# An attention and gated feed-forward kernel: the planner counts TensorE's waits as instructions, and works the order out anew

## The chip, the cores and the metric

The kernel runs on one core of one Trainium2 chip. The metric is device microseconds of one execution. Before the change three runs took 560.89, 561.74 and 563.44 us, median 561.74. A further execution was profiled: it took 564.12 us itself, and its span, from the first to the last instruction, is 562.3 us.

## The reference

Eight batches, eight heads, head size 64. 512 local positions see each other in a band and 32 global positions in full; the global positions see everything. The result, transposed to 576 x 512 per batch, goes through a product with a 512 x 1024 weight, a convolution of three taps along the sequence as a gate, and a product with a 1024 x 512 weight.

```python
s_g = scale * q_g @ k_all.T            # 32 global queries, all 544 keys
out_g = softmax(s_g) @ v_all
s_ll = where(abs(i - j) <= 32, scale * q_l @ k_l.T, -1e9)
s_l = concat([scale * q_l @ k_g.T, s_ll])
out_l = softmax(s_l) @ concat([v_g, v_l])
x = transpose(concat([out_g, out_l]))   # batch, 576, 512
h = max(x @ w_in, 0)
conv = sum(conv_w[k] * shifted(h, k - 1) for k in range(3))
out = (h * sigmoid(conv)) @ w_out
```

All of it is fp32. The weights come as float64.

## The kernel before

**Attention.** Heads go in pairs, 32 pairs in all, four to a batch. A step is one function call for one pair, head or group, and the planner names it by a letter. S (`SC`, line 270) makes the scores of a pair with 64 small matmuls of 32 columns of weights each (in the first batch also two masks by line 275). M, NM, E, NS, NP and TD are maximum, scaling, exponential, sums, division and a 32 x 32 transposition on VectorE, ScalarE or GpSimd. P (`PV`, line 367) multiplies by the values with 104 small matmuls; UA copies the result out of PSUM. Once a batch the global queries take G (line 296, 48 small matmuls), GM, GE, GN, GT (transpositions, lines 426 and 427), GC, GP (line 441, 80 small matmuls), GD, GX and GO.

**Feed-forward.** It goes in nine chunks: the 512 local columns of each batch, and a last one with the 35 columns a batch that are left (280). A chunk has eight Z steps (`PZ`, line 476): each is 12 matmuls of 128 x 512, four blocks of channels times three products of split operands. In chunk 0 a Z step is 4 plain fp32 matmuls (line 471, eight records). RE, C1, Ca, Cb, TH, GG, GH and GL are rectifier, convolution, tanh gate and split of the result on ScalarE and VectorE. Four output blocks follow, each in two halves Oa and Ob (line 530) of 12 full-width matmuls. OE copies an output block to SBUF and ST stores it. The float64 weights, eight loads of 1024 KB (WD), are turned into fp32 and split by WA, WB, WC, WH and WL in the first part of the kernel. A load of a pair's queries and keys (LQ) has 704 KB, one of its values (LV) 448 KB.

**The order.** Nothing is ordered by hand. `plan` (line 696) lists all steps with costs, buffers and dependences, and gives each a due time: TensorE steps from `attention` and `feed` (lines 782 and 790), which read the table TIME, plus a shift from POS0 (first batch and weights), POS1 (second batch) or POS; other steps from what needs them, less SLACK times the costs between, plus a shift. `arranged` (line 863) plays the five engines' queues through in time: whenever an engine is free it takes the ready step with the earliest due time for which the buffers are free. The start times so found give the order, which `emit` (line 954) writes out and fixes on every engine. So the numbers in the tables change the order and nothing else of the program.

**TensorE's program as the planner sees it.** Every matmul has a weight load as an instruction of its own. `INSTR` (line 685) and `instructions` (line 689) give the number of instructions of a step: 128 for S, 208 for P, 96 for G, 160 for GP, 24 for a full-width group of 12 matmuls. In `arranged` (lines 922 to 928) the program is cut in blocks of 256, the first boundary at 190. Some instructions ahead of a boundary the fetch of the block after it is begun; it is there some time later, and a step that reaches a boundary before its block is there is late by the difference. Separate waits (`EVENT_SEMAPHORE`), which the compiler puts into TensorE's program where an instruction waits for more than it can name, are not counted.

Of the kernel before, what the change touches and what calls it, by code (L numbers as in the profile page):

```python
# [19 lines left out]
P = 128  # L20
H = 8
SL = 512
SG = 32
S = SL + SG
# [39 lines left out]
def attn_moe(ctx: ExitStack, tc: tile.TileContext, qk_d, vw_d, qg_d, w_in_d, w_out_d, cw_d, out_d):  # L64
# [269 lines left out]

    def NP(n):
        p, r = heads[n]["p"], heads[n // 2 * 2]["r"][:, n % 2]
        if choice("NP") == "a":
            for t in range(4):
                nc.scalar.activation(out=p[:, t], in_=p[:, t], func=AF.Copy, scale=r[:, t : t + 1])  # L339
        else:  # L340
            eng("NP").tensor_tensor(out=p, in0=p, in1=r[:, :, None].to_broadcast([P, 4, P]), op=ALU.mult)

# [33 lines left out]

    def XE(n):
        b, h = divmod(n, H)
# [42 lines left out]

    def GT(n):
        gr = groups[n // 4]
# [115 lines left out]
    def ST(o):  # L539
# [9 lines left out]
    emit(tc, B, dict(  # L549
        LQ=LQ, LV=LV, LG=LG, G=G, S=SC, M=MA, NM=NM, E=EX, NS=NS, NP=NP, TD=TD, P=PV, UA=UA, XE=XE, XH=XH, XL=XL,  # L550
        GM=GM, GE=GE, GN=GN, GT=GT, GC=GC, GP=GP, GD=GD, GX=GX, GO=GO,
# [12 lines left out]
ENG = dict(  # L564
    GC="a", GO="a", NP="a", XH="a", XL="p", NM="a", RE="a", C1="a", GH="v", GL="v", OE="v", UA="a", GD="a",
    WH="a", WL="v",
)
ENG0 = dict(
    GC="a", GO="a", NP="p", XH="a", XL="v", NM="a", RE="a", C1="a", GH="a", GL="v", OE="a", UA="a", GD="a",
    WH="a", WL="v",  # L570
)

POS = dict(
    XE=-1.98, LQ=-80.99, LG=-87.83, LV=71.12, S=-17.28, M=-27.44, E=-6.13, NS=-3.92, NM=23.86, P=1.39, UA=-4.24,
    NP=31.47, TD=-5.07, XH=-12.07, XL=10.02, G=52.87, GM=29.81, GE=-37.35, GN=-115.2, GD=105.99, GX=29.95,
    GT=129.43, GC=-31.93, GP=-26.41, GO=-8.78, PZ=14.19, RE=-3.14, C1=2.98, Ca=0.43, Cb=0.55, TH=9.34, GG=-5.2,
    GH=8.26, GL=-12.28, Oa=61.51, Ob=-1.61, OE=61.39, ST=-10.74, WD=-19.78, TP=-9.03, WA=-50.95, WB=133.34, WC=0.26,
    WH=37.69, WL=-74.11,
)
POS0 = dict(  # L580
    XE=71.87, LQ=7.24, LG=-63.06, LV=45.31, S=126.77, M=-117.38, E=8.85, NS=-300.71, NM=-150.66, P=-86.58,
    UA=-59.52, NP=-71.33, TD=-53.52, XH=39.01, XL=-39.39, G=-5.17, GM=-83.24, GE=24.98, GN=-203.07, GD=23.65,
    GX=12.62, GT=31.6, GC=-44.1, GP=68.52, GO=-255.02, PZ=107.21, RE=31.17, C1=13.3, Ca=-9.79, Cb=-16.57, TH=-79.02,
    GG=-97.16, GH=-0.63, GL=9.06, Oa=110.77, Ob=0.43, OE=-108.95, ST=93.13, WD=-24.99, TP=-179.51, WA=78.67,
    WB=8.55, WC=-17.88, WH=37.31, WL=7.82,
)
POS1 = dict(
    XE=-150.52, LQ=4.25, LG=21.89, LV=64.47, S=-102.2, M=55.36, E=-44.06, NS=-77.31, NM=-31.46, P=51.55, UA=-82.55,
    NP=17.29, TD=-25.06, XH=12.69, XL=-16.47, G=199.57, GM=-62.58, GE=148.46, GN=17.3, GD=81.6, GX=-42.37,
    GT=112.38, GC=-31.9, GP=-31.58, GO=-202.72, PZ=98.05, RE=-16.73, C1=124.35, Ca=-6, Cb=127.63, TH=14.86,  # L590
    GG=160.89, GH=79.39, GL=44.16, Oa=-177.1, Ob=11.66, OE=142.4, ST=7.86, WD=-94.15, TP=28.9, WA=53.39, WB=-5.7,
    WC=103.86, WH=35.99, WL=96.74,
)

TIME = dict(
    A0=35.78, R0=-44.3, A1=35.35, R1=-21.21, A2=113.9, R=14.48, PER=62.4, T0=117.37, Z0=-24.44, O0=74.74, OR0=9.08,
    T1=118.03, ZR=178.55, OD=30.59, OR=19.82, END=-27.04,
)
MASKED = 1
SLACK = 2.092  # L600

WAYS = {}

# [1 line left out]
def cost(key, e, long=LONG):  # L605
# [45 lines left out]
    if key == "C1":  # L651
        return act(n, more=93) if e == "a" else fast(n) if e == "v" else pool1(n)
    return dict(
        LQ=dma(704), LV=dma(448), LG=dma(64), WD=dma(1024), ST=(900, 2400),
        S=pe(940), SM=pe(1400), M0=(690, 770), XE=(110, 140), TD=(590, 670), P=pe(1430), G=pe(940), GT=pe(500), GP=pe(1190), GX=pe(150),
        PZ=group(), Oa=group(), Ob=group(), F=pe(3540),
# [18 lines left out]
    p=("S", "G", "GT", "P", "GP", "GX", "PZ", "Oa", "Ob"), s=("LQ", "LV", "LG", "WD", "ST"),  # L675
    a=("E", "GE", "TH", "WA"), g=("XE",),
)
PE, DVE, ACT, POOL, SP = range(5)
# [4 lines left out]


INSTR = dict(S=128, P=208, G=96, GT=10, GP=160, GX=2)
FETCH = (190, 3400, 64)


def instructions(key, i):

    if key == "PZ" and i < NFT:
        return 16
    return INSTR.get(key, 24) + 4 * (key == "S" and i < H * MASKED)


def plan(B):
# [166 lines left out]
def arranged(ops):  # L863

    free = {k: v for k, v in SLOTS.items()}
    free["h"], free["o_"], free["at"] = LIMIT["h"], LIMIT["o"], LIMIT["at"]
    kind, left, gone = {}, {}, {}
    for key, i, e, c, takes, uses, before, pos, later in ops:
        for k, name in takes:
            kind[name] = k  # L870
            left[name] = left.get(name, 0) + 1
        for name in uses:
            left[name] = left.get(name, 0) + 1
    after = [[] for _ in ops]
    waits = [0] * len(ops)
    for j, o in enumerate(ops):
        waits[j] = len(o[6])
        for x in o[6]:
            after[x].append(j)
    ready = [0] * len(ops)  # L880
    queue = [[] for _ in range(5)]
    for j, o in enumerate(ops):
        if not waits[j]:
            queue[o[2]].append(j)
    until, shared, mode = [0] * 5, 0, 0
    begun, bound, trigger, there, coming = 0, FETCH[0], FETCH[0] - FETCH[2], 0, 0
    start = [None] * len(ops)
    events, done, now = [0], 0, -1
    frees = []
    while events:  # L890
        t = heapq.heappop(events)
        if t == now:
            continue
        now = t
        while frees and frees[0][0] <= t:
            free[heapq.heappop(frees)[1]] += 1
        for e in (PE, DVE, ACT, POOL, SP):
            if until[e] > t:
                continue
            best = None  # L900
            for j in queue[e]:
                o = ops[j]
                at = o[7] - (STAY if e == PE and mode and MODE.get(o[0], 0) == mode else 0)
                if ready[j] > t or (best is not None and (at, j) >= best):
                    continue
                if (e == POOL or (e == DVE and o[0] in SHARED)) and shared > t:
                    continue
                need = {}
                for k, _ in o[4]:
                    need[k] = need.get(k, 0) + 1  # L910
                if all(free[k] >= v for k, v in need.items()):
                    best = (at, j)
            if best is None:
                continue
            j = best[1]
            key, i, _, (occ, lat), takes, uses, before, pos, later = ops[j]
            queue[e].remove(j)
            if e == PE:
                m = MODE.get(key, 0)
                if m != mode:  # L920
                    occ, lat, mode = occ + SWITCH[m > 0], lat + SWITCH[m > 0], m
                count, late = instructions(key, i), 0
                while min(trigger, bound) < begun + count:
                    at = t + late + occ * (min(trigger, bound) - begun) // count
                    if trigger < bound:
                        coming, trigger = max(at, there) + FETCH[1], trigger + 256
                    else:
                        late, there, bound = late + max(there - at, 0), coming, bound + 256
                begun, occ, lat = begun + count, occ + late, lat + late
            start[j] = t  # L930
            done += 1
            until[e] = t + occ
            heapq.heappush(events, t + occ)
            if e == POOL or (e == DVE and key in SHARED):
                shared = t + occ
            for k, _ in takes:
                free[k] -= 1
            for name in [x for _, x in takes] + list(uses):
                gone[name] = max(gone.get(name, 0), t + lat)
                left[name] -= 1  # L940
                if not left[name]:
                    heapq.heappush(frees, (gone[name] + 60, kind[name]))
                    heapq.heappush(events, gone[name] + 60)
            for x in after[j]:
                ready[x] = max(ready[x], t + lat + (20 if ops[x][2] == e else 100 if ops[x][2] == POOL else 45))
                waits[x] -= 1
                if not waits[x]:
                    queue[ops[x][2]].append(x)
                    heapq.heappush(events, max(ready[x], t))
    assert done == len(ops), [ops[j][:2] for q in queue for j in q]  # L950
    return start, max(s + o[3][1] for s, o in zip(start, ops))
# [73 lines left out]
```

## Time and profile before

| | |
|---|---|
| three runs | 560.89, 561.74, 563.44 us |
| profiled execution, its own time | 564.12 us |
| its span | 562.3 us |
| TensorE busy with matmuls | 528.6 us, 94% |
| TensorE weight loads (beside them) | 414.3 us, 74% |
| VectorE busy | 421.8 us, 75% |
| ScalarE busy | 373.8 us, 66% |
| GpSimd busy | 71.7 us, 13% |
| matmuls, weight loads | 8192, 8192 |
| mean granted clock of TensorE | 0.969 |
| data moved by the DMA engines | 56.83 MB |
| packets of the two instruction queues | 64 (1.05 MB) and 21 (0.17 MB) |

The profile is of one execution. "busy" is the union of an engine's instructions in time. A granted clock of 1 is 2.4 GHz and 0.5 is 1.2 GHz. "issue" as the cause of idle time means that the engine waited for no semaphore that the profile shows. In a row of waits the numbers are us in total, times, and the longest. PE is TensorE, PEld its weight loads, DVE VectorE, ACT ScalarE, POOL GpSimd, SP the engine that issues the loads and stores.

### The profile page before, as it was taken

How to read it: one execution, taken by the hardware profiler on the slowest of the kernel's cores; microseconds unless marked ns; L12 is line 12 of the kernel's file. 1: busy time of each engine (PE TensorE's matmuls, PEld its weight loads, DVE VectorE, ACT ScalarE, POOL GpSimd, SP SyncE). 2: the span in 40 equal slices, each digit the busy share in tenths (PEclk: the TensorE clock that was granted, in tenths of full speed). 3: DMA queues.
4: the chain of work that ended last, by engine and by line, in shares of the span. 5: the costliest groups of instructions: out<-in, count | busy, mean ns of one | idle time of the engine just before them, and what ended most of it. 6: DMA issues, size and time to landing. Idle time of an engine off the chain costs nothing.

```text
span 562.3 us, 19172 instructions
## 1 busy us (share of the span) xinstructions
PE 528.6 (94%) x8192; PEld 414.3 (74%) x8192; DVE 421.8 (75%) x796; ACT 373.8 (66%) x1262; POOL 71.7 (13%) x98
## 2 busy tenths in 40 slices
PE   5779899998999998999999998999899999999996
PEld 3465366787778886787878886877777788888895
DVE  2897999998888786674787766897758659667562
ACT  4867976778876794769676784879538865433230
POOL 4412321001210012000400022001300031101000
PEclk9658999999999999999999998999999999999999
DMA  8992651142222304222050404240030000000112
GB/s 344 417 358 77 230 189 64 54 141 94 100 89 72 115 30 151 76 97 100 23 188 38 175 3 152 71 174 23 26 113 21 4 35 6 37 20 19 39 39 38
DMA packets 20517, 56.83 MB, mean 101 GB/s; under 512 B 6096, under 2 KB 11216, under 8 KB 19408
## 3 DMA queue, kind: packets, MB, share of 16 engines
q1 hardware_dynamic: 20432, 55.61, 27.5%
q8 instruction: 64, 1.05, 0.8%
q14 instruction: 21, 0.17, 0.1%
HBM read 46.69 MB, written 8.91 MB: 99 GB/s over the span
## 4 chain that ended last, share of the span: by engine, by line
PE 83%; DVE 8%; issue 3%; ACT 3%; DMA 1%; POOL 0%; DVEq 0%; ACTq 0%; POOLq 0%
PE ps_o L530 33%; PE ps_h L476 29%; PE ps_v L367 8%; PE ps_s L270 6%; PE ps_h L471 2%; PE go L441 2%; DVE negm L304 1%; DVE pt L326 1%; PE psg L296 1%; DVE t L496 1%; PE gt L426 1%; ACT pr L339 1%; DMA qk<-qk 1%; ACT pr L316 1%; DVE ps_s L303 1%
## 5 line engine op out<-in xcount | busy, mean ns | idle before, releaser
L530 PE MATMUL ps_o<-g,wh 128*128 128x512 f32 (+1 forms) x576 | 186.6, 392 | 0.0
L496 DVE SCALAR_TENSOR_TENSOR t<-h,cw,t 128x511 f32<-128x511 f32 (+1 forms) x144 | 104.2, 734 | 29.6 <-ACT t L250 28.6
L530 PEld LDWEIGHTS ps_o<-g,wh 128*128 128x128 f32 x576 | 108.0, 190 | 23.6 <-issue 0.8
L530 PE MATMUL ps_o<-g,wl 128*128 128x512 f32 (+1 forms) x288 | 111.0, 385 | 0.0
L476 PE MATMUL ps_h<-h,wh 128*128 128x512 f32 (+1 forms) x256 | 100.9, 394 | 0.0
L476 PE MATMUL ps_h<-h,wl 128*128 128x512 f32 (+1 forms) x256 | 98.0, 383 | 0.0
L476 PE MATMUL ps_h<-l,wh 128*128 128x512 f32 (+1 forms) x256 | 97.5, 381 | 0.0
L316 ACT ACTIVATE pr<-ps_s,negm 128x128 f32<-128x128 f32 x256 | 90.1, 369 | 1.7 <-DVE pt L326 0.7
L484 ACT ACTIVATE h<-ps_h 128x512 f32<-128x512 f32 (+1 forms) x72 | 41.7, 580 | 52.6 <-PE ps_h L476 45.5
L367 PEld LDWEIGHTS ps_v<-pt,vf 32*64 32x64 f32 x3328 | 51.2, 140 | 24.3 <-issue 12.2
L502 ACT ACTIVATE t<-t 128x512 f32<-128x512 f32 (+1 forms) x72 | 44.0, 612 | 34.8 <-DVE t L496 32.4
L367 PE MATMUL ps_v<-pt,vf 32*64 32x64 f32 (+3 forms) x3328 | 57.4, 254 | 10.1 <-issue 5.9
L530 PEld LDWEIGHTS ps_o<-g,wl 128*128 128x128 f32 x288 | 54.7, 190 | 10.8
L326 DVE STREAM_TRANSPOSE pt<-pr 128x512 f32<-128x512 f32 x64 | 44.7, 703 | 23.4 <-ACT pr L339 21.5
L339 ACT ACTIVATE pr<-pr,sums 128x128 f32<-128x128 f32 x192 | 60.8, 407 | 1.7 <-DVE sums L333 1.7
L506 DVE SCALAR_TENSOR_TENSOR t<-t,h 128x512 f32<-128x512 f32 (+1 forms) x72 | 52.8, 742 | 12.1 <-ACT t L502 11.8
L250 ACT ACTIVATE t<-h,cw 128x512 f32<-128x512 f32 (+1 forms) x72 | 50.5, 706 | 13.1 <-DVE g L220 12.4
L476 PEld LDWEIGHTS ps_h<-h,wh 128*128 128x128 f32 x256 | 48.1, 188 | 11.9 <-issue 1.6
L476 PEld LDWEIGHTS ps_h<-h,wl 128*128 128x128 f32 x256 | 48.1, 188 | 10.4
L476 PEld LDWEIGHTS ps_h<-l,wh 128*128 128x128 f32 x256 | 48.1, 188 | 9.3
L304 DVE TENSOR_REDUCE negm<-ps_s 128x4 f32<-128x512 f32 x64 | 44.0, 691 | 12.9 <-PE ps_s L275 10.3
L316 ACT ACTIVATION_READ_ACCUMULATOR pr<-ps_s,negm 128x1 f32 x256 | 53.4, 208 | 0.0
(74 smaller groups left out, 580.0 us busy)
## 6 DMA issues: line engine op xcount, KB each, us to landing
qk<-qk SPq DMA_DIRECT2D x32, 704.0 KB, 6.0
vf<-vw SPq DMA_DIRECT2D x32, 448.0 KB, 4.5
out<-o SPq DMA_DIRECT2D x32, 255.5 KB, 2.0
raw<-w_in SPq DMA_DIRECT2D x4, 1024.0 KB, 11.3
raw<-w_out SPq DMA_DIRECT2D x4, 1024.0 KB, 7.0
out<-o SPq DMA_DIRECT2D x4, 132.0 KB, 3.2
qgf<-qg SPq DMA_DIRECT2D x8, 64.0 KB, 5.7
cwr<-cw SPq DMA_DIRECT2D x1, 24.0 KB, 10.0
```

The costliest lines, as they stand in the source:

```text
L250: nc.scalar.activation(out=out, in_=in_, func=AF.Copy, scale=by)
L304: nc.vector.tensor_reduce(out=st["m"], in_=st["s"], axis=mybir.AxisListType.X, op=ALU.max)
L316: nc.scalar.activation(out=st["p"][:, t, :], in_=st["s"][:, t, :], func=AF.Exp, scale=SCALE, bias=st["m"][:, t : t + 1], accum_out=two["r" ...
L326: nc.vector.transpose(out=st["pt"][:, n % 2].rearrange("p t k q -> p (t k q)"), in_=heads[n]["p"].rearrange("p t k -> p (t k)"))
L339: nc.scalar.activation(out=p[:, t], in_=p[:, t], func=AF.Copy, scale=r[:, t : t + 1])
L367: nc.tensor.matmul(x, lhsT=v, rhs=p, start=k == 0, stop=k == len(work[j, b]) - 1)
L476: nc.tensor.matmul(st["z"][:, 0:n], lhsT=w_in(w, ft, ct), rhs=x[part], start=i == 0, stop=i == 3 * NCT - 1)
L484: nc.scalar.activation(out=h[:, 0:n], in_=z[:, 0:n], func=AF.Relu, scale=0.5)
L496: nc.vector.scalar_tensor_tensor(out=t, in0=h, scalar=cw[:, 3 * ft + k : 3 * ft + k + 1], in1=t, op0=ALU.mult, op1=ALU.add)
L502: nc.scalar.activation(out=t, in_=t, func=AF.Tanh)
L506: nc.vector.scalar_tensor_tensor(out=t, in0=t, scalar=1.0, in1=h, op0=ALU.add, op1=ALU.mult)
L530: nc.tensor.matmul(ps, lhsT=w_out(w, mt, ft), rhs=g, start=ft + i == 0, stop=ft == NFT - 1 and i == 2)
```

## The change

The count of a step's instructions gets one more in P, G and GP steps and in every third of the others. A fetch is taken to last 3450 instead of 3400 ns, or 5500 ns if the queue of loads is still busy in the plan up to 1500 ns before the time at which the fetch begins, and it begins 50 instead of 64 instructions ahead of the boundary. The tables POS, POS0, POS1, TIME and SLACK have new numbers, so the order of all steps on all engines is new. The steps themselves, the buffers, the costs and the engines that they run on stay as they are.

```diff
--- before.py
+++ after.py
@@ -571,33 +571,33 @@
 )
 
 POS = dict(
-    XE=-1.98, LQ=-80.99, LG=-87.83, LV=71.12, S=-17.28, M=-27.44, E=-6.13, NS=-3.92, NM=23.86, P=1.39, UA=-4.24,
-    NP=31.47, TD=-5.07, XH=-12.07, XL=10.02, G=52.87, GM=29.81, GE=-37.35, GN=-115.2, GD=105.99, GX=29.95,
-    GT=129.43, GC=-31.93, GP=-26.41, GO=-8.78, PZ=14.19, RE=-3.14, C1=2.98, Ca=0.43, Cb=0.55, TH=9.34, GG=-5.2,
-    GH=8.26, GL=-12.28, Oa=61.51, Ob=-1.61, OE=61.39, ST=-10.74, WD=-19.78, TP=-9.03, WA=-50.95, WB=133.34, WC=0.26,
-    WH=37.69, WL=-74.11,
+    XE=-40.21, LQ=155.99, LG=44.21, LV=48.17, S=94.27, M=-3.78, E=2.16, NS=-1.35, NM=-2.21, P=-1.79, UA=5.89,
+    NP=-1.47, TD=1.18, XH=-2.94, XL=4.6, G=134.07, GM=50.45, GE=-31.52, GN=-23.16, GD=37.91, GX=-54.56, GT=-11.1,
+    GC=26.27, GP=-0.81, GO=229.47, PZ=33.3, RE=-2.63, C1=-3.89, Ca=4.61, Cb=3.23, TH=-1.63, GG=2.68, GH=-2.01,
+    GL=-2.31, Oa=-12.37, Ob=3.86, OE=-44.57, ST=-7.64, WD=-61.54, TP=3.93, WA=163.45, WB=-95.99, WC=55.97,
+    WH=186.14, WL=-46.68,
 )
 POS0 = dict(
-    XE=71.87, LQ=7.24, LG=-63.06, LV=45.31, S=126.77, M=-117.38, E=8.85, NS=-300.71, NM=-150.66, P=-86.58,
-    UA=-59.52, NP=-71.33, TD=-53.52, XH=39.01, XL=-39.39, G=-5.17, GM=-83.24, GE=24.98, GN=-203.07, GD=23.65,
-    GX=12.62, GT=31.6, GC=-44.1, GP=68.52, GO=-255.02, PZ=107.21, RE=31.17, C1=13.3, Ca=-9.79, Cb=-16.57, TH=-79.02,
-    GG=-97.16, GH=-0.63, GL=9.06, Oa=110.77, Ob=0.43, OE=-108.95, ST=93.13, WD=-24.99, TP=-179.51, WA=78.67,
-    WB=8.55, WC=-17.88, WH=37.31, WL=7.82,
+    XE=-29.14, LQ=-45.12, LG=-169.65, LV=13.98, S=-8.27, M=-87.9, E=-21.95, NS=32.88, NM=27.73, P=76.08, UA=-13.17,
+    NP=13.23, TD=-13.91, XH=-13.93, XL=76.42, G=13.87, GM=-34.75, GE=-12.19, GN=33.78, GD=-85.95, GX=1.77,
+    GT=-97.72, GC=5.1, GP=24.67, GO=-100.45, PZ=2, RE=-8.58, C1=69.32, Ca=72.28, Cb=-17.55, TH=-30.35, GG=-6.29,
+    GH=-31.2, GL=-3.32, Oa=-20.38, Ob=3.35, OE=-9.78, ST=40.96, WD=-45.63, TP=35.8, WA=3.99, WB=-10, WC=5.61,
+    WH=-10.47, WL=1.6,
 )
 POS1 = dict(
-    XE=-150.52, LQ=4.25, LG=21.89, LV=64.47, S=-102.2, M=55.36, E=-44.06, NS=-77.31, NM=-31.46, P=51.55, UA=-82.55,
-    NP=17.29, TD=-25.06, XH=12.69, XL=-16.47, G=199.57, GM=-62.58, GE=148.46, GN=17.3, GD=81.6, GX=-42.37,
-    GT=112.38, GC=-31.9, GP=-31.58, GO=-202.72, PZ=98.05, RE=-16.73, C1=124.35, Ca=-6, Cb=127.63, TH=14.86,
-    GG=160.89, GH=79.39, GL=44.16, Oa=-177.1, Ob=11.66, OE=142.4, ST=7.86, WD=-94.15, TP=28.9, WA=53.39, WB=-5.7,
-    WC=103.86, WH=35.99, WL=96.74,
+    XE=-29.02, LQ=-26.54, LG=-11.72, LV=93.31, S=58.42, M=37.61, E=-2.61, NS=11.38, NM=-11.02, P=-15.31, UA=34.12,
+    NP=-6.55, TD=-11.58, XH=50.36, XL=-98.13, G=55.74, GM=-84.06, GE=76.43, GN=-59.12, GD=-20.14, GX=97.12,
+    GT=-18.53, GC=-1.63, GP=155.32, GO=89.44, PZ=-12.58, RE=59.82, C1=198.55, Ca=75.2, Cb=83.72, TH=-29.44,
+    GG=168.39, GH=-55.2, GL=-1.43, Oa=156.85, Ob=-9.56, OE=-16.45, ST=145.12, WD=-48.91, TP=92.07, WA=-133.55,
+    WB=-219.38, WC=287.43, WH=-48.95, WL=-54.48,
 )
 
 TIME = dict(
-    A0=35.78, R0=-44.3, A1=35.35, R1=-21.21, A2=113.9, R=14.48, PER=62.4, T0=117.37, Z0=-24.44, O0=74.74, OR0=9.08,
-    T1=118.03, ZR=178.55, OD=30.59, OR=19.82, END=-27.04,
+    A0=9.42, R0=27.75, A1=43.69, R1=6.01, A2=101.89, R=15.35, PER=63.73, T0=-59.35, Z0=160.71, O0=74.51, OR0=21.33,
+    T1=104.58, ZR=114.59, OD=23.52, OR=13.58, END=-16.52,
 )
 MASKED = 1
-SLACK = 2.092
+SLACK = 2.025
 
 WAYS = {}
 
@@ -683,14 +683,15 @@
 
 
 INSTR = dict(S=128, P=208, G=96, GT=10, GP=160, GX=2)
-FETCH = (190, 3400, 64)
+FETCH = (190, 3450, 50, 5500)
 
 
 def instructions(key, i):
 
+    waits = key in ("P", "G", "GP") or i % 3 == 0
     if key == "PZ" and i < NFT:
-        return 16
-    return INSTR.get(key, 24) + 4 * (key == "S" and i < H * MASKED)
+        return 16 + waits
+    return INSTR.get(key, 24) + 4 * (key == "S" and i < H * MASKED) + waits
 
 
 def plan(B):
@@ -923,7 +924,8 @@
                 while min(trigger, bound) < begun + count:
                     at = t + late + occ * (min(trigger, bound) - begun) // count
                     if trigger < bound:
-                        coming, trigger = max(at, there) + FETCH[1], trigger + 256
+                        at = max(at, there)
+                        coming, trigger = at + FETCH[3 if until[SP] + 1500 > at else 1], trigger + 256
                     else:
                         late, there, bound = late + max(there - at, 0), coming, bound + 256
                 begun, occ, lat = begun + count, occ + late, lat + late
```

## Rows read from the trace of the kernel before

**Rows 1.** The page's first section: busy us, share of the span, instructions.

```profile
PE 528.6 (94%) x8192; PEld 414.3 (74%) x8192; DVE 421.8 (75%) x796; ACT 373.8 (66%) x1262; POOL 71.7 (13%) x98
```

**Rows 2.** By stretch: length, busy (count) of PE, PEld, DVE, ACT, POOL, clock, DMA, GB/s.

```profile
0.00:44.00 44.00, 29.14 (x856) 21.00 (x856) 28.85 (x62) 28.82 (x121) 15.30 (x34) 0.71 0.93 361
...
84.00:546.00 462.00, 451.94 (x6534) 361.78 (x6533) 350.53 (x653) 309.98 (x1032) 45.38 (x53) 0.99 0.21 73
546.00:562.35 16.35, 10.84 (x84) 10.61 (x83) 4.79 (x11) 1.38 (x3) 0.00 (x0) 0.96 0.21 33
...
343.00:346.00 3.00, 3.00 (x14) 2.25 (x9) 1.15 (x2) 1.74 (x4) 0.56 (x2) 0.50 0.65 189
```

**Rows 3.** TensorE's waits from 84 us on: us in all, times, longest.

```profile
PE ps_s L270 <- issue: 5.0, 3, 2.6
PE go L441 <- issue: 3.3, 2, 1.8
PE ps_v L367 <- issue: 1.5, 1, 1.5
PE ps_v L367 <- DVE o L217: 0.3, 1, 0.3
```

**Rows 4.** TensorE in time order: start, us, work; in brackets idle before.

```profile
134.70 0.24 PE L367 MATMUL ps_v<-pt,vf 32*64 32x32 f32 x1 [1.47 <-issue]
...
218.27 1.57 PE L367 MATMUL ps_v<-pt,vf 32*64 32x128 f32 x104
219.77 1.11 PE L270 MATMUL ps_s<-qk 64*32 64x128 f32 x59
223.52 0.64 PE L270 MATMUL ps_s<-qk 64*32 64x128 f32 x5 [2.64 <-issue]
...
435.93 0.87 PE L270 MATMUL ps_s<-qk 64*32 64x128 f32 x41 [1.09 <-issue]
```

**Rows 5.** By stretch as rows 2, cut at the ends of stops.

```profile
14.10:134.65 120.55, 107.88 (x2032) 74.17 (x2031) 109.60 (x208) 94.23 (x316) 22.40 (x25) 0.89 0.49 183
150.45:223.50 73.05, 70.39 (x1145) 56.14 (x1145) 58.96 (x109) 51.60 (x177) 8.87 (x11) 1.00 0.26 89
14.10:435.92 421.82, 400.53 (x6866) 307.43 (x6866) 338.75 (x648) 311.88 (x1074) 55.29 (x64) 0.96 0.32 115
```

**Rows 6.** Separate waits in TensorE's program, of the P step's line.

```profile
L367 PEldq EVENT_SEMAPHORE  x52: 51/51/51, 17.7 to 458.5; - x52
```

**Rows 7.** Instruction packets: 0 to 44, 84 to 546, 220.8 to 223.6 us.

```profile
q8 instruction: 6, 0.10, 0.9%
...
q8 instruction: 52, 0.85, 0.8%
...
q8 instruction: 1, 0.02, 2.2%
```

**Rows 8.** The chain that ended last: start, us, what.

```profile
215.34 3.00 PE ps_o L530 x12
...
224.16 4.11 PE ps_o L530 x12
...
235.20 2.80 PE ps_o L530 x12
...
343.24 4.30 PE ps_o L530 x12
```

**Rows 9.** TensorE's waits up to 84 us; then the first feed-forward group.

```profile
PE ps_s L270 <- DMA qk<-qk: 5.0, 1, 5.0
PE ps_v L367 <- issue: 4.4, 4, 2.6
PE ps_v L367 <- ACT pr L316: 2.6, 3, 1.4
PE ps_s L270 <- issue: 1.9, 1, 1.9
...
44.67 4.18 PE L471 MATMUL ps_h<-x,wf 128*128 128x512 f32 x8
```

## The prediction, on record before the result

> **What bounds the kernel now.** I read the engine shares first. TensorE is busy for 528.6 of the 562.3 us [rows 1]; VectorE has 421.8 and ScalarE 373.8 us, so only TensorE's sum is near the span. The table by stage [rows 2] then splits TensorE's missing 33.7 us: 14.9 us are missing in the first 44 us, 10.1 in the 462 us between 84 and 546, 5.5 after 546, and so 3.2 between 44 and 84. The granted clock says the same: 0.71 in the first 44 us, 0.99 from 84 to 546, where 1 is 2.4 GHz. So the kernel has an opening of some 84 us with several limits, then a long stretch that TensorE fills, then a short tail.
>
> In the long stretch the waits of TensorE [rows 3] show almost one cause. It waited 0.3 us for VectorE, once, and 9.8 us in six gaps that end with "issue", that is, with no semaphore that the profile shows. Three of the six stand in [rows 4], and all look alike: two or three of the steps with many small matmuls stand directly behind each other (a P step of 104 matmuls, then an S step of 64, in the row that has its run-up), and the engine stops inside one of them: 1.47, 1.28, 2.64, 1.80, 1.52 and 1.09 us in order of time, 9.80 in all.
>
> Why there? Count the instructions from one stop to the next [rows 5]. From 150.45 to 223.50 us there are 1145 matmuls and 1145 weight loads, 2290; 9 x 256 is 2304, 14 more. From the first 256-instruction boundary at which it stops, at 14.1 us, to the first of the six, the sum falls short of 16 x 256 by 33; in the remaining four stretches it does so by 3, 25, 13 and 4. The missing instructions are the separate waits in TensorE's program: there are 104 of them in the whole kernel, by nine rows of which the largest stands in [rows 6], and the shortfalls sum to 92 by 436 us: 2 x 6866 = 13732 against 54 x 256 = 13824 over all six stretches together. So the six stops stand on one grid of 256 instructions, waits included. In the 2.8 us around the 2.64 us stop the DMA records hold just one packet of the instruction queue, of 0.02 MB [rows 7]: the engine stood at the end of a block of its program while the next was being fetched.
>
> The Trainium skill ("Runtime: NRT & Kernel Launch", section "Instruction fetch mechanics") has the same block of 256 instructions, 16 KiB, but says that crossing a boundary is mostly hidden because instructions are dispatched more slowly than fetched. By that rule the gaps would be something else, and a corrected count would save nothing. The trace disagrees with it for runs of small matmuls (2.64 us lost at one boundary) and agrees for the other boundaries, since 52 blocks came between 84 and 546 us [rows 7], and 46 of them cost nothing.
>
> **The planner's old count and the new one.** The old planner has this mechanism already, without the waits: its boundaries drift away from the true ones, by as many instructions as there were waits before. At the six stops those are 33, 36, 50, 75, 88 and 92, by summing [rows 5]. What was left of the run of small matmuls at each stop was 1, 7, 5, 27, 13 and 41 matmuls [rows 4], twice as many instructions: 2, 14, 10, 54, 26, 82. Each is smaller than the drift. So at all six the old planner believed that the boundary lay behind the run, in a full-width group, where 24 instructions last 2.8 us and a fetch is covered. The six stops are not bad luck in the durations; they are the counting error. The new rule adds one for each P, G and GP step and for every third of the other steps: 32 + 8 + 8, and 11 S, 6 GT, 3 GX, 24 PZ, 12 Oa and 12 Ob, 116 in all against 104 measured. The drift shrinks from 104 to about 12 at the end.
>
> **The terms**, against the profiled execution's own 564.12 us (the span and 1.8 us around it). No instruction of the computation is added or removed; the order and the places of the waits change.
>
> 1. The six stops: -9.8 us if none returns. The engine stops where some 300 small instructions stand together (163 matmuls and their loads, 326, before the 2.64 us stop [rows 4]), and the planner can now see which boundaries fall so.
> 2. The clock behind them. Behind the two longest stops it fell: it is 0.50, that is 1.2 GHz, from 343 to 346 us [rows 2], behind the 1.80 us stop. There a group of 12 matmuls took 4.30 us and behind the 2.64 us stop 4.11, where such a group behind small matmuls takes 3.00 [rows 8]. That is 1.1 + 1.3 = 2.4 us, gone with the stops: -2.4.
> 3. Stops that return: a count off by up to 12, and a fetch that can last longer than planned. From 0 to all of terms 1 and 2 (12.2); I take one of six at its mean, +1.6, since the error left is an eighth of the old one.
> 4. Keeping such steps apart. A full-width group lasts 2.80 us behind another and 3.00 behind small matmuls [rows 8], so each run that is broken up costs 0.20 us. Bounds: nothing (runs moved to another place) to 32 P steps apart, 6.4 us; six runs, +1.2.
> 5. The opening, whose order is wholly new: the first parameter set (POS0) and the first chunks' times change by tens of units. TensorE waits there 6.3 us on "issue", 5.0 us for the first load, and 6.8 us on ScalarE and VectorE, in six rows of which the largest stands in [rows 9]. The wait for the first load stays: what TensorE needs first is still a pair's queries and keys. The fetch part should shrink with the new 5.5 us under loads, but the DMA engines are 0.93 busy and only 6 blocks came in the first 44 us [rows 2, 7], 7 us each, which is more than 5.5; and a step freed from the fetch meets the ScalarE and VectorE waits next. Bounds: -6.3 (all of its fetch waits) to +18 (as much again as the 18.1 us that TensorE misses up to 84 us). I take 0, between small gains and small losses, because nothing in the trace shows which way a new order of this stretch goes.
> 6. The waits on other engines between 84 and 546 us: 0.3 us before. TensorE is covered because VectorE is busy 350.5 of 462 us there and ScalarE 310.0 [rows 2], so each has slack, and the planner's costs for them held. 0; if that cover goes, each late result costs what such waits cost in the opening, up to some 0.9 us (2.6 us in three times, [rows 9]).
> 7. The tail, 5.5 us without matmuls at the end, is the last copies and two stores behind each other; the order of the last steps hardly differs in kind. 0, give or take 1.
>
> Sum: -9.8 - 2.4 + 1.6 + 1.2 = -9.4, so 554.7 for the profiled execution. That execution was 2.4 us above the median of the three runs shown (561.74), so the median goes to 552.3; I write 552.4.
>
> **Rivals.**
> The opening gets longer (slower). The place is the first group of chunk 0, which starts at 44.67 us [rows 9] and needs four pairs' attention and the first weights. Loads come at 361 GB/s [rows 2], so each load of 1024 KB that the new order puts ahead of what this group needs moves it 2.9 us. From 3.2 such loads on (9.4 us) all of the gain is gone; with five, four weight loads and more than a pair's queries and keys, it is 14.5 us, and the time 561.7 - 9.4 + 14.5 = 567. For it: the new settings turn the sequence of the first attention pairs round (R0 from -44 to +28). Against it: the old opening was no better ordered by any row that I can see.
>
> The gain is there but is eaten, or the stops only move: the longer fetch time in the plan makes the scheduler hold small-matmul steps back, their results come late, and TensorE waits for ScalarE and VectorE as it does in the opening (6.8 us), plus two of the six stops at 1.6. -9.4 + 6.8 + 3.2 = +0.6, or 562.3, no change. That the change doesn't do what it says belongs here: waits are given to steps by a rule, not read from the program, and 52 of the 104 stand at the P line alone [rows 6], where the rule gives 32, so the boundaries could be off by more in some stretch.
>
> By the rule of a hidden fetch the "issue" gaps come from elsewhere and stay: 561.7 as well, by 9.8 us that do not move. The block grid of [rows 5] speaks against it.
>
> The opening gains too: its 6.3 us go and the first group comes earlier by as much: 552.4 - 6.3 = 546.1.
>
> **Chances and range.** Forecast, from 548 to 557 by itself: 0.60. Opening gains too: 0.11. No change: 0.12, and 0.02 for the hidden fetch, of which I count 0.01 with the faster. Slower: 0.15. About 0.5% (2.8 us) is what a measurement of this kernel can tell from no change. Faster by more is the forecast and the good opening, 0.72; within it 0.13; slower 0.15. The range reaches down to the good opening and up to the edge of no change: 545.5 to 561.5, with some 0.05 below and 0.15 to 0.2 above.
>
> **What the profile after would show.** Right: between 84 and 546 us TensorE's "issue" waits fall from 9.8 to under 3 us; the granted clock there is 1.00 in nearly all slices; boundaries, counted with waits, fall in full-width groups or behind a single small-matmul step; waits for other engines stay under 2 us. Term 4: the number of full-width groups of 3.00 us rises by a few. Term 5 is read from TensorE's missing time in the first 84 us, 18.1 now, and from the start of the first group, 44.67. The prediction is wrong if gaps of over 1 us on "issue" remain in several adjacent small-matmul steps (the count doesn't do it), or if that stretch is clean and the time is still above 559 (the opening, then, or new waits).

## The result, and the profile after

The changed kernel takes 553.52 us (median; 552.89 to 556.25) against 561.35 for the kernel before on the same chip (560.89 to 563.44): the ratio is 0.9863, with a 95% interval of 0.9821 to 0.9904. The forecast was 552.4 (545.5 to 561.5), so its size was right. On a second chip the pair took 554.77 and 565.53 us, 0.9791 [0.9761, 0.9820]; between these two chips the kernel before differs by 4.18 us and the changed one by 1.25, so every experiment below is compared with runs of the kernel before beside it.

The profiled execution took 552.89 us, its span 551.1 against 562.35: 11.2 us less. The page's busy row and its row of the granted clock in 40 slices:

```profile
PE 527.6 (96%) x8192; PEld 411.5 (75%) x8192; DVE 416.1 (76%) x796; ACT 372.7 (68%) x1262; POOL 69.3 (13%) x98
...
PEclk9569979999999999999999999999999999999999
```

TensorE's busy time fell by only 1.1 us, from 528.6 [rows 1]; 10.2 us of the 11.2 are idle time that is gone. Where, the table by stretch of the kernel after says (columns as in [rows 2]):

```profile
0.00:44.00 44.00, 29.61 (x805) 20.84 (x805) 31.14 (x59) 27.23 (x105) 15.52 (x34) 0.77 0.84 338
44.00:84.00 40.00, 36.55 (x686) 19.58 (x686) 39.31 (x74) 32.53 (x113) 12.16 (x10) 0.91 0.44 157
84.00:535.00 451.00, 451.00 (x6638) 360.91 (x6627) 341.64 (x656) 311.97 (x1042) 41.63 (x54) 1.00 0.21 78
535.00:551.10 16.10, 10.41 (x81) 10.19 (x79) 4.02 (x9) 0.97 (x2) 0.00 (x0) 0.93 0.24 46
```

Read the busy figure against the length. From 84 to 535 us TensorE is busy for all of 451.00 us, at clock 1.00; before, 10.1 us were missing in the corresponding stretch, at 0.99 [rows 2]. TensorE's list of waits has no row from 84 us on, where [rows 3] had four. Up to 84 us 14.4 + 3.4 = 17.8 us are missing (18.1 before), and in the tail 5.7 (5.5 before). The opening is as long but made differently; its largest waits in the kernel after are (us in all, times, longest):

```profile
PE ps_s L270 <- DMA qk<-qk: 5.1, 1, 5.1
PE ps_v L367 <- issue: 4.1, 2, 2.6
PE ps_s L270 <- issue: 2.1, 2, 1.8
PE ps_v L367 <- DVE sums L332: 1.4, 1, 1.4
PE ps_h L471 <- DVE wf L199: 1.3, 1, 1.3
```

Against [rows 9], the wait for the first load is the same (5.1), the fetch waits are 6.9 us in all with a row of 0.7 not shown (6.3 before), and waits for ScalarE and VectorE go on beside them. The first feed-forward group starts 4 us earlier than in [rows 9], which brought nothing to the end; in TensorE's order of time it is

```profile
40.56 3.70 PE L471 MATMUL ps_h<-x,wf 128*128 128x512 f32 x8
```

The chain of the kernel after, in a stretch that has its longest run of small matmuls from 84 us on (a GP, an S and a GX step, 146 matmuls and their loads, at 185.69 us; start, us, what):

```profile
185.69 1.25 PE go L441 x80
186.94 1.09 PE ps_s L270 x64
188.03 0.37 PE gx L455 x2
188.40 2.81 PE ps_h L476 x12
191.20 1.50 PE ps_v L367 x71
192.70 3.00 PE ps_h L476 x12
195.70 2.80 PE ps_o L530 x12
198.50 2.03 PE ps_s L270 x124
200.53 3.00 PE ps_h L476 x12
```

Two S steps (128 matmuls, 256 instructions) stand together; no P step stands directly in front of an S step here, as at 218 us in [rows 4]. Groups of 12 take about 2.80 or 3.00 us, none the 4.11 and 4.30 of [rows 8]. Counted in the two traces from 84 us on (matmuls and weight loads), the old order has ten runs of 336 to 384 small-matmul instructions in a row, the new one none above 292. Runs of full-width matmuls that stand behind an S, P, G or GP step, and take the 0.20 us more of [rows 8], went from 38 to 45; behind a transposition (lines 427 and 455) neither trace shows that price, as in the group at 188.40.

One execution of an experiment, the profiled one of the new tables with the old model, took 623.3 us at a granted clock of 0.83 where the other eleven took 568.3 to 572.3, and the ratio is without it.

### The profile page after: what moved, and what is told of

Its sections match the earlier page's. It is cut to its first block, busy times and chain, and to the rows that moved or that the text cites. A ratio compares the mean times of both kernels' runs of the same rounds, so it can differ in the third digit from the quotient of the medians.

```text
span 551.1 us, 19168 instructions
## 1 busy us (share of the span) xinstructions
PE 527.6 (96%) x8192; PEld 411.5 (75%) x8192; DVE 416.1 (76%) x796; ACT 372.7 (68%) x1262; POOL 69.3 (13%) x98
## 4 chain that ended last, share of the span: by engine, by line
PE 87%; DVE 10%; issue 1%; DMA 1%; ACT 0%; DVEq 0%
PE ps_o L530 35%; PE ps_h L476 32%; PE ps_v L367 8%; PE ps_s L270 6%; PE ps_h L471 2%; PE go L441 2%; DVE pt L326 1%; PE psg L296 1%; PE gt L426 1%; DVE negm L304 1%; DVE t L496 1%; DVE wf L119 1%; DVE wf L199 1%; DMA qk<-qk 1%; DVE wf L114 1%
## 5 line engine op out<-in xcount | busy, mean ns | idle before, releaser
L530 PE MATMUL ps_o<-g,wh 128*128 128x512 f32 (+1 forms) x576 | 184.2, 388 | 0.0
L496 DVE SCALAR_TENSOR_TENSOR t<-h,cw,t 128x511 f32<-128x511 f32 (+1 forms) x144 | 109.3, 762 | 23.6 <-ACT t L250 22.5
L530 PEld LDWEIGHTS ps_o<-g,wh 128*128 128x128 f32 x576 | 106.4, 188 | 22.8 <-issue 0.2
L476 PE MATMUL ps_h<-h,wh 128*128 128x512 f32 (+1 forms) x256 | 102.2, 399 | 0.0
L217 DVE COPY o<-ps_o 128x512 f32<-128x512 f32 (+1 forms) x32 | 21.1, 660 | 57.9 <-PE ps_o L530 55.2
L367 PE MATMUL ps_v<-pt,vf 32*64 32x64 f32 (+3 forms) x3328 | 55.2, 252 | 6.8 <-issue 4.1
L339 ACT ACTIVATE pr<-pr,sums 128x128 f32<-128x128 f32 x192 | 59.3, 409 | 0.0
L506 DVE SCALAR_TENSOR_TENSOR t<-t,h 128x512 f32<-128x512 f32 (+1 forms) x72 | 48.8, 679 | 11.2 <-ACT t L502 10.2
## 6 DMA issues: line engine op xcount, KB each, us to landing
cwr<-cw SPq DMA_DIRECT2D x1, 24.0 KB, 10.1
```

The costliest lines, as they stand in the source:

```text
L367: nc.tensor.matmul(x, lhsT=v, rhs=p, start=k == 0, stop=k == len(work[j, b]) - 1)
L476: nc.tensor.matmul(st["z"][:, 0:n], lhsT=w_in(w, ft, ct), rhs=x[part], start=i == 0, stop=i == 3 * NCT - 1)
L496: nc.vector.scalar_tensor_tensor(out=t, in0=h, scalar=cw[:, 3 * ft + k : 3 * ft + k + 1], in1=t, op0=ALU.mult, op1=ALU.add)
L506: nc.vector.scalar_tensor_tensor(out=t, in0=t, scalar=1.0, in1=h, op0=ALU.add, op1=ALU.mult)
L530: nc.tensor.matmul(ps, lhsT=w_out(w, mt, ft), rhs=g, start=ft + i == 0, stop=ft == NFT - 1 and i == 2)
```

## The experiments

The changed kernel differs in three things: the tables (POS, POS0, POS1, TIME, SLACK), the count of instructions, and the fetch time (5500 ns under loads; the 3400 to 3450 and 64 to 50 beside it). They were taken apart both ways, and the block grid was moved by itself. In the edits, "old" and "new" are the lines of the diff above.

**The new tables under the old model.** The old FETCH, `instructions` and trigger line, all else as changed:

```
-FETCH = (190, 3450, 50, 5500)
+FETCH = (190, 3400, 64)
-    waits = key in ("P", "G", "GP") or i % 3 == 0
...
-                        coming, trigger = at + FETCH[3 if until[SP] + 1500 > at else 1], trigger + 256
+                        coming, trigger = max(at, there) + FETCH[1], trigger + 256
```

> New tables (POS, POS0, POS1, TIME, SLACK), but the old count without waits, the old fetch of 3400 ns begun 64 instructions ahead, no longer fetch under loads. Theory A (the tables alone do it: their order never puts more than about 300 small instructions together, so hardly any boundary can stop TensorE): no more than one stop of about 1.4 us after 84 us, time 553 to 556. Rival B (the corrected count and fetch do it): the stops come back, four to six of them, 5 to 10 us, time 559 to 563.

Measured: 570.44 us, ratio 1.0091 [1.0059, 1.0124]. Neither theory foresaw a slower kernel. So the tables have no worth of their own: under the old model they give a slower order, though one without fetch waits after 84 us.

**The old tables with the new count.** Before, plus the new `instructions`:

```
+    waits = key in ("P", "G", "GP") or i % 3 == 0
-        return 16
-    return INSTR.get(key, 24) + 4 * (key == "S" and i < H * MASKED)
+        return 16 + waits
+    return INSTR.get(key, 24) + 4 * (key == "S" and i < H * MASKED) + waits
```

> Old tables, old fetch, but waits counted by the new rule; the steps then start at other times in the plan and the order changes a little. Theory A (tables): counting right lets the plan see a stop but not avoid it; by counting the compiled program's instructions I expect four or five stops after 84 us, 5 to 8 us together, at small-matmul runs near 133, 160, 342 and 402 us; time 556 to 561. Rival B (the count): at most one stop, time 551 to 554.

Measured: 558.49 us, 0.9883 [0.9838, 0.9928]. TensorE's waits from 84 us on (us in all, times, longest):

```profile
PE go L441 <- issue: 2.7, 2, 1.8
PE ps_s L270 <- issue: 1.4, 1, 1.4
PE ps_v L367 <- issue: 1.2, 1, 1.2
PE ps_o L530 <- issue: 1.0, 1, 1.0
```

One of these stops in the same kernel, with TensorE in time order:

```profile
332.89 1.57 PE L367 MATMUL ps_v<-pt,vf 32*64 32x128 f32 x104 [0.27 <-DVE o L217]
334.39 0.98 PE L441 MATMUL go<-vf,pgt 128*32 128x64 f32 x53
336.33 0.64 PE L441 MATMUL go<-vf,pgt 128*32 128x64 f32 x27 [0.96 <-issue]
```

Five stops, 6.3 us, are still there, behind small steps that stand directly behind each other, as before. So a planner that counts the waits doesn't keep these steps apart. The gain of this order is 3.5 us of shorter stops and, by term 2, 2.4 of clock (it is 1.00 from 44 to 552 us). The prediction's theory, that the count removes the stops, falls here. The code has the reason: `arranged` chooses the next step by due time and free buffers, and only then are `instructions` and FETCH used, to make the chosen step end later. A right count tells the planner of a stop but doesn't let it choose another step there.

**The block grid moved, both orders.** A step of 16 matmul calls on the identity (64 instructions, result unused) is put at the very start; the order behind it is untouched, but every 256-instruction boundary falls 64 instructions earlier in it:

```
+    def PAD(n):
+        t = bank([P, 4, P], "ps_pad")
+        for _ in range(n):
+            nc.tensor.matmul(t[0:SG, 0], lhsT=ident[0:D, 0:SG], rhs=ident[0:D, :], start=True, stop=True)
...
+    todo = [("PAD", 16, 0)]
```

> The old order step for step, with 64 more TensorE instructions (32 small matmuls on the identity, results unused) while it waits for the first load; every boundary then falls 64 instructions earlier in the work. Theory (the six stops are block boundaries at unlucky places of long runs of small matmuls): all six go or fall under 0.2 us, one new one of about 1.3 us comes near 455 us, TensorE's issue waits after 84 us fall from 9.8 to 1 to 3 us, the clock stays at 1.00 and the time is 549.5 to 553. Rival (the stops belong to those steps or to transfers at that time, not to the 256 grid): six stops at the same steps, time 561 to 562.

Measured with the order before: 561.52 us, 0.9928 [0.9892, 0.9963]. Of the six old stops four are gone, that at 150 us has 0.30 left, and the 2.64 us one moved to another place of the same run. From 84 us on:

```profile
PE ps_s L270 <- issue: 3.1, 2, 2.8
PE go L441 <- issue: 2.2, 2, 1.2
PE ps_h L476 <- issue: 0.5, 1, 0.5
```

That is 5.8 us for 9.8. The last two rows are three stops at places that were free before (though the run of the 1.24 us one, at 86 us, had a stop of 0.44 us at 81 us in the old grid). The largest of all, in time order:

```profile
223.94 1.57 PE L367 MATMUL ps_v<-pt,vf 32*64 32x128 f32 x104
225.44 0.65 PE L270 MATMUL ps_s<-qk 64*32 64x128 f32 x27
228.90 1.49 PE L270 MATMUL ps_s<-qk 64*32 64x128 f32 x37 [2.81 <-issue]
230.32 0.79 PE L530 MATMUL ps_o<-g,wh 128*128 128x512 f32 x1
```

The stretches around it, by the table (columns as in [rows 2]; the last two are the DMA engines' busy share and GB/s):

```profile
222.00:226.00 4.00, 4.00 (x140) 3.15 (x139) 2.42 (x3) 0.67 (x4) 0.95 (x2) 1.00 0.94 306
226.00:229.00 3.00, 0.19 (x13) 0.10 (x15) 0.00 (x0) 0.72 (x2) 1.26 (x1) 0.88 0.81 279
229.00:235.00 6.00, 6.00 (x48) 4.62 (x48) 2.16 (x4) 3.31 (x18) 0.00 (x0) 0.50 0.03 9
```

The boundary now lies 32 matmuls earlier in the S step, 27 instead of 59 in, as 64 instructions make it, and the stop didn't shrink with it. Loads kept the DMA engines 0.94 and 0.81 busy around it, as they did at the old stop (0.70 in the 2.8 us of [rows 7]). Five other boundaries of this run have about as many small instructions ahead of them (239 to 279, counted in the compiled program; this one 264) and DMA engines at most 0.27 busy in the 5 us before: they cost 0 to 0.30 us. So the stops belong to the grid, and by this comparison, which no run tests by itself, how long one lasts also depends on loads. Behind the stop the clock is at 0.50, its 1.2 GHz level, for all of the next 6 us.

The time missed my 549.5 to 553; it lies in the rival's 561 to 562, but the rival's sign, six stops at the same steps, did not show. The added matmuls delay the opening themselves:

```profile
3.03 6.82 PE L552 MATMUL ps_pad<-ident 64*32 64x128 f32 x31 [3.03 <-POOL ident L83]
9.43 0.46 PE L270 MATMUL ps_s<-qk 64*32 64x128 f32 x7
```

They take 0.2 us each, and the first S step starts at 9.43 us instead of 5.00. The same matmul of the work, the 600th before, starts at 41.1 us instead of 33.8.

> The new order step for step with the same 64 more TensorE instructions ahead. Theory A (no run in the new order is long enough, wherever a boundary falls): no issue wait after 84 us, time 552.5 to 555. Rival B (the new order has long runs, but the right count has put every boundary at a harmless place): shifted by 64, three to six stops return, 4 to 9 us, time 557 to 562.

Measured with the changed order: 557.51 us, 0.9862 [0.9821, 0.9904]. No wait of TensorE after 84 us (busy 56.00 of 56 and 395.00 of 395, clock 1.00):

```profile
84.00:140.00 56.00, 56.00 (x835) 42.52 (x834) 53.52 (x93) 43.40 (x133) 6.53 (x6) 1.00 0.28 100
140.00:535.00 395.00, 395.00 (x5875) 317.08 (x5874) 290.86 (x575) 271.08 (x915) 38.21 (x50) 1.00 0.22 80
```

At this place of the grid, too, the new order has no stop. The time is 2.5 us above what I expected; against the changed kernel the delay is all in the opening, behind the added matmuls (the 1700th matmul of the work ends 3.8 us later, the last 3.9).

**The changed kernel without the load term.**

```
-FETCH = (190, 3450, 50, 5500)
+FETCH = (190, 3450, 50, 3450)
```

> The changed kernel with one number altered: a fetch under loads takes 3450 ns in the plan like any other, not 5500. The order that comes out is the same as with the old count and the old fetch (the run with new tables and old model). Theory A (the load term is what keeps the plan of the opening true; without it steps are put in an order that the opening can't follow): slower than before by 0.5 to 1.3%, no issue waits of note after 84 us, but 4 us or more of waits for ScalarE and VectorE there, and a clock that falls between 80 and 140 us. Rival B (that run was slow for a reason of the chip, such as its clock): time 0.983 to 0.990 of before.

Measured: 570.04 us, 1.0069 [1.0034, 1.0103]. Slower than before, and in the same order, instruction for instruction, as the new tables under the old model. What the two kernels lack in common is the 5500. All its waits of TensorE from 84 us on:

```profile
PE ps_s L270 <- ACT pr L316: 3.7, 1, 3.7
PE ps_v L367 <- ACT pr L316: 3.1, 3, 1.9
PE ps_o L530 <- ACT pr L316: 1.1, 1, 1.1
PE ps_h L471 <- DVE wf L199: 0.7, 1, 0.7
PE ps_o L530 <- DVE g L220: 0.4, 1, 0.4
```

The stretches in which they fall; the third busy column is VectorE's:

```profile
84.00:100.00 16.00, 15.26 (x194) 9.35 (x184) 15.93 (x22) 9.10 (x14) 0.77 (x1) 1.00 0.25 87
100.00:110.00 10.00, 6.29 (x134) 4.36 (x133) 9.79 (x19) 6.47 (x25) 0.00 (x0) 0.66 0.25 93
110.00:120.00 10.00, 8.54 (x36) 6.30 (x35) 9.86 (x16) 7.92 (x31) 0.00 (x0) 1.00 0.07 28
120.00:130.00 10.00, 6.91 (x176) 5.15 (x181) 7.79 (x16) 9.45 (x47) 0.88 (x1) 0.85 0.25 85
```

The rows name ScalarE's `pr`, but up to 120 us ScalarE is not full; VectorE is, with 35.6 of the 36 us, and the chain of waits of this kernel runs on VectorE from 88 to 125 us (weight splits, convolution, softmax maxima) and only then through `pr` to TensorE. The opening itself is no longer (16.6 us missing up to 84). Of the 17.3 us over the changed kernel's span, 9.0 are these waits, 9.4 more busy time of TensorE (537.0), in part at the clock of 0.66 to 0.85 of these rows, and -1.3 the opening. A full VectorE alone is not the reason: in the changed kernel it is busy for 9.83 and 9.87 us of the two stretches from 100 to 120 us, and TensorE waits for nothing. But there it had done 70.4 us of work by 84 us, here 67.8. So the load term, the one number that differs, changes the order of VectorE's work in and behind the opening; which step of that order makes the difference, no run singles out. That is not what I had weighed it for.

**The load term alone.** Before, plus the new FETCH and trigger line:

```
-FETCH = (190, 3400, 64)
+FETCH = (190, 3450, 50, 5500)
...
+                        at = max(at, there)
+                        coming, trigger = at + FETCH[3 if until[SP] + 1500 > at else 1], trigger + 256
```

> Old tables and the old count, but the fetch as the changed kernel plans it: 3450 ns, 5500 under loads, begun 50 instructions ahead. Theory A (the load term makes the plan of the opening true, whatever the tables): waits for ScalarE and VectorE before 84 us fall below the old 6.8 us; by counting the compiled program, four stops after 70 us (near 85, 93, 330 and 430 us), 4 to 7 us; ratio to before 0.980 to 0.990. Rival B (the load term only helps with the tables that were found with it): opening as before or worse, ratio 0.993 to 1.01.

Measured: 557.26 us, 0.9835 [0.9806, 0.9864]. Three stops of 2.9 us in all remain after 84 us where four of 4 to 7 us were expected, the clock is 1.00 there, and the other waits of the opening are 7.1 us, not less, so my account of how it helps there missed while the ratio came out. By itself it gives 1.65 per cent, where the whole change run beside it gives 2.09.

**That order with the grid moved.** The same, with the PAD step at 12 calls (48 instructions), where the count says that fewer of its boundaries fall behind a long run:

> The order of old tables with the new fetch, step for step, and 48 more TensorE instructions ahead, which moves its block boundaries. By the grid theory one stop of 1.4 us is left after 70 us (near 93 us) of four, so 2 to 5 us less than without: 0.972 to 0.984 of before, which would beat the changed kernel, since it also changes 57 times between small matmuls and full-width groups where the changed kernel does 64 times. If something else decides (the opening), it stays within 0.3% of the same order without them.

Measured: 558.89 us, 0.9864 [0.9831, 0.9897]. All stops are gone (no "issue" row after 84 us), also the one that I had expected to be left near 93 us. So the places of the boundaries can be predicted, but not each stop: one boundary with 422 small instructions ahead of it, at 105 us, cost nothing, and neither did the same one with 470 ahead in the run before. The opening is again about 4 us longer (1700th matmul of the work at 102.3 us against 98.6), and the time is 1.6 us longer, not the 2 to 5 us shorter that I expected.

**The changed kernel without the new count, twice.** The old `instructions`, all else as changed:

```
-    waits = key in ("P", "G", "GP") or i % 3 == 0
-        return 16 + waits
-    return INSTR.get(key, 24) + 4 * (key == "S" and i < H * MASKED) + waits
+        return 16
+    return INSTR.get(key, 24) + 4 * (key == "S" and i < H * MASKED)
```

> The changed kernel with the old count (no waits), its fetch times and tables kept. Theory A (with these tables the count hardly matters, since no run of small matmuls is long enough; the load term and the tables carry the gain): ratio to before 0.983 to 0.990, at most one stop after 84 us. Rival B (the count is needed): three or more stops, 4 us or more, ratio 0.993 to 1.00.

Measured: 553.25 us, 0.9765 [0.9711, 0.9820], faster than expected, one stop of 0.4 us after 84 us. Repeated on one chip beside the changed kernel:

> The changed kernel with the old count (no waits) again, beside the changed kernel on one chip. Theory A (with these tables the waits in the count are worth nothing): within 0.4% of the changed kernel, no stop above 0.5 us after 84 us. Rival B: the changed kernel is faster by 0.5% or more.

> The changed kernel once more, on the chip of the three runs beside it, as their measure: 0.980 to 0.990 of before, no issue waits after 84 us.

Measured: 553.43 us, 0.9767 [0.9739, 0.9796], and 554.77, 0.9791 [0.9761, 0.9820], a little under the 0.980 expected. The intervals overlap, and the old count is 1.3 us the faster, less than the 0.5% (2.8 us) that I can tell from no change: with these tables the waits in the count are worth nothing that can be measured, and neither kernel of this pair waits after 84 us. The stretch behind the opening, in the kernel with the old count:

```profile
84.00:140.00 56.00, 56.00 (x741) 43.38 (x740) 53.61 (x88) 44.01 (x140) 4.50 (x4) 1.00 0.19 68
```

And in the changed kernel beside it, TensorE also busy for all of 56 us at clock 1.00:

```profile
84.00:140.00 56.00, 56.00 (x762) 43.48 (x747) 52.45 (x82) 42.93 (x137) 3.24 (x4) 1.00 0.18 61
```

**The opening's fetch waits.** Are its 6.9 us of "issue" caused by the loads, and would their end help? Each of the first 24 loads is made to wait for the load two before it, then for the one four before:

```
+            if key in ("LQ", "LV", "LG", "WD"):
+                loads.append(ins)
+                if 2 < len(loads) < 24:
+                    tc.add_manual_dep(
+                        ins, loads[-1 - 2].name,
+                        mybir.DependencyInfo(mybir.DependencyClass.Sync, mybir.DependencyReason.DATA), reason="pace",
+                    )
```

> The changed kernel, each of the first 24 loads waiting until the load two before it has landed, so that at most two are in flight instead of up to eight. Same order on every engine. Theory A (a fetch lasts long in the opening because its packet stands behind loads already issued): the issue waits before 84 us fall from 6.9 to under 3.5 us, and with them the time, to 0.975 to 0.984 of before. Rival B (the fetch waits only hide ScalarE, VectorE and landing waits that come next): issue waits fall too, but the waits on others grow by as much; ratio 0.984 to 0.992. Rival C (a fetch under loads is slow by shared bandwidth, not by a queue): issue waits stay at 6 us or more.

> The changed kernel, each of the first 24 loads waiting until the load four before it has landed (two before it in the earlier run, up to eight in flight without). Theory A (fewer loads ahead of a fetch packet shorten the opening's fetch waits, and with four in flight no load comes late): issue waits before 84 us of 4 to 6 us instead of 7.3, waits for loads no more than 5.5 us, ratio to before 0.970 to 0.978, better than the changed kernel. Rival B (the fetch waits in the opening cover waits for ScalarE, VectorE and loads that come next): issue waits fall but the stretch up to 84 us misses 17 to 19 us of TensorE as before; ratio 0.978 to 0.985.

Measured: 558.59 us, 0.9837 [0.9782, 0.9891], and 555.90, 0.9811 [0.9767, 0.9855]. Up to 84 us, the loads paced two deep:

```profile
PE ps_s L270 <- DMA qk<-qk: 6.9, 4, 5.1
PE ps_v L367 <- DMA vf<-vw: 3.9, 1, 3.9
PE ps_v L367 <- ACT x L217: 2.8, 2, 2.4
PE psg L296 <- issue: 1.3, 1, 1.3
...
PE ps_s L270 <- issue: 1.2, 1, 1.2
...
PE ps_v L367 <- issue: 1.0, 1, 1.0
```

Two deep, the fetch waits halve (3.5 us), but the data come later by more, and 21.1 us are missing up to 84 instead of 17.8. Four deep they don't fall at all (9.1 us, where 4 to 6 were expected). So whether the loads cause them stays open: two deep, the longer waits for data may just cover them. What is seen is that less of one wait came with more of the others, as the prediction's fifth term had it; neither run is clearly faster than the changed kernel.

## Why the prediction was right, and where its reason was wrong

Term 1, the six stops: -9.8 forecast; the stretch's missing time went from 10.1 to 0. Term 2, the clock behind them: no group of 4.11 or 4.30 us is left, in line with -2.4. Term 3, stops that return: +1.6 allowed, none came back, also not with the grid moved. Term 4, the switches: seven more instead of six, which at the 0.20 us of [rows 8] is +1.4 for +1.2. TensorE's busy time agrees: -2.4 + 1.4 = -1.0 against -1.1 measured. Term 5, the opening: 0 forecast, -0.3 measured. Terms 6 and 7: 0.3 us of waits became none, and the tail is 0.2 longer. So the ledger, -10.1 for the long stretch, -0.3 and +0.2 for opening and tail, -1.1 for busy time, gives the measured -11.2 within rounding. Forecast was -9.4; the difference is term 3's allowance of 1.6 and 0.4 of terms 5 to 7, less term 4's 0.2. The median came out 1.1 us above the forecast, not below, because I took 2.4 off for the distance of the profiled execution from it, and the profiled execution after is 0.6 below its median.

The sum held, but the sentence "they are the counting error" failed. What it rests on holds: the stops stand on one grid of 256 instructions with waits counted, since shifting the grid by 64 and by 48 instructions moved, shortened or removed all nine, though not each as expected, and counted in the compiled programs every "issue" stop after 84 us, in all of the runs, begins within ten instructions behind a boundary. The leap was from "the planner has the boundary in the wrong place" to "with it in the right place the planner will avoid them". With the new count alone it left 6.3 us in five stops, and with the new tables and load term but without it only 0.4 us came back, once in two runs. The new count isn't exact either: the changed kernel's program has 129 separate waits, the rule gives 116. What removes the stops is that the new order has no small-step run as long as those that stopped. Counted in the compiled programs, the six old stops had 302 to 342 small instructions in a row ahead of their boundary and the five with the new count alone 313 to 369; in the new order, as it is, with the grid moved and with the old count, no boundary after 84 us had more than 230. That no boundary anywhere in its run of 292 would stop it is not shown. So the -9.8 came out for another reason than the one given; as far as the prediction's reasoning goes, that is luck. Accordingly the sign that I had named, boundaries in full-width groups or behind a single small step, did not show: in the order after they fall in P, S, GP and full-width steps alike, and cost nothing in any.

This also puts the rule weighed in the prediction in its place. The Trainium skill ("Runtime: NRT & Kernel Launch", section "Instruction fetch mechanics") calls crossing a block "mostly hidden"; in the order after that held for all of the blocks that came between 84 and 535 us (53 packets of the instruction queue). Of all the stops over 0.5 us after 84 us, in every run here, one alone had fewer than 302 small instructions ahead of its boundary: the 2.81 us one beside loads, with 264.

How the gain divides: the parts don't add. Beside the kernel before, the count alone gives 0.9883, the load term alone 0.9835, the new tables alone 1.0091, tables with count 1.0069, tables with load term 0.9765 and 0.9767, all three 0.9863 and 0.9791. Each set of tables goes with the model that it stands under: the term that I had weighed as a possible help to the opening, and put at nothing, is the one without which these tables lose. No experiment clearly beat the changed kernel. Left open: whether the new tables could have been found without the corrected count, and the old tables with count and load term together, which wasn't run.

## What to carry to other kernels

Where an engine stops for its own instructions, first prove the grid: count instructions and separate waits from stop to stop, then shift everything by a few dozen instructions and see whether the stops move. Then look for an order that has no run of tiny instructions as long as those that stop, rather than for a planner that knows where the boundaries are but can't choose by it. A planner's tables and its cost model are one object: taking one part of such a change alone can turn a gain into a loss.

## What the runs showed of the hardware that was not expected

The length of a fetch stop alone does not tell whether TensorE's clock falls behind it. It fell to 0.50 behind stops of 2.64, 1.80 and 2.81 us, and none of the five stops of 0.95 to 1.77 us in the kernel with the old tables and the new count took it below 1.00; but in the old order with the grid moved it was 0.57 on average from 88 to 92 us, 2 us behind the stop of 1.24. With loads in flight the same boundary cost more than its place explains: moved 32 matmuls earlier in its step, the 2.64 us stop became 2.81 at 279 to 306 GB/s. And a small matmul is not always cheap: the 32 added at the start took 0.2 us each, where the row at 223.94 us has 104 in 1.57 us. All of the added ones write the same place of PSUM (`t[0:SG, 0]`), unlike those of the S and P steps; that this is why is not tested.
